# One wide product for high and low rows in the last wide expert of an attention, MoE and MLP kernel

## The chip, the core and the metric

The kernel runs on one core of a Trainium2 chip. The metric is the device time of one execution in microseconds (us). TensorE multiplies matrices and writes its results to PSUM; ScalarE and VectorE read PSUM and do the elementwise work; GpSimd issues the gathers and scatters; SyncE issues the weight loads. Each engine works through its own instructions in the order in which they were issued and waits on semaphores for the others.

## The reference

Attention over a window of 64 positions (2 batches, 8 heads, 576 positions, head size 64) gives 1152 rows of 512 values. Each row goes to the one of 8 experts that its gate chooses, then all rows go through a second MLP:

```python
logits = x @ w_gate
expert_idx = np.argmax(logits, axis=1)
...
h = np.maximum(np.einsum('ecd,edf->ecf', disp, w1), 0.0)
y = np.einsum('ecf,efd->ecd', h, w2)
...
out[i] = gate_w[i] * y[expert_idx[i], pos[i]]
```

```python
h = x @ w_in
g = np.maximum(h, 0.0) + alpha * np.minimum(h, 0.0)
return (g @ w_out).astype(np.float32)
```

An expert has 1024 hidden units and a capacity of 288 rows; the second MLP has 2048 hidden units. All arrays are float32. With the reference's own inputs the experts get, from the largest, 254, 234, 220, 194, 123, 74, 42 and 11 rows.

## The kernel before

**Numbers in two parts.** A float32 factor is held as a high part, rounded to the type `float32r`, and a low part, the remainder. A product of two such factors is the sum of three matmuls: high by high, high by low and low by high. `mm3` (L216) issues the three; `wide_up` writes its three out at L1092.

**Experts.** The experts are taken in an order of their size; `room` (L55) is how many rows each gets in the main path, and rows beyond that go to the part behind `tc.If(n_over > 0)` (L1439), which ends with a second pass of the second MLP. The experts with more than 128 rows of room are "wide" (positions 1, 3 and 7), the others "narrow"; positions 5 and 6 (`PAIR`) share one run of matmuls on unsplit weights. Position 7 (`HOST`, the fourth largest) is computed last, and the steps of the pair (the generator `pair`, L1237) run in between its own.

**A wide expert.** `halves_of` (L1160) turns its rows around into `xt`, high and low part, with columns for rows. `wide_up` (L1084) goes through four chunks of weights; a chunk has two blocks `f` of 128 hidden units, each the sum over four slices `kk` of three products. Both blocks of a chunk stand in one PSUM tile `hps` of the pool `ps_h` (two buffers, which `sps` of the narrow experts and `py` of the pair share). ScalarE makes the high part `hh` with a Relu out of PSUM (L1102), VectorE the low part `hl` (L1103). `wide_down` (L1112) sums four output blocks `y` over four chunks and two `f`; `put` (L1120) copies one block into its window of `x2`, the input of the second MLP: ScalarE casts the high part (L1121), VectorE subtracts for the low part (L1122). The window's place is known only at run time.

**Work issued in between.** The order of instructions is the order of the program (`tc.manual_schedule`). `prepare` (L1074) splits the next 128x1024 chunk of expert weights: a cast to `whi` (L1078, on ScalarE, each fourth one on VectorE) and a subtraction to `wlo` (L143, VectorE), after which the raw buffer is free and SyncE may issue the next load into it. `cvt_tick` (L193) does the same for a piece of the second MLP's weights, which come as pairs of 32-bit words: on ScalarE `mag` (L165) and a cast (L188), on VectorE L172, L173, L176 and L189. In `HOST` it is called after each chunk of `wide_up` and after the first three of `wide_down`; its first call that does anything is the one after chunk 2, and issues two `mag` activations, for the first two pieces. The later calls issue one tick each.

**Order in `HOST`.** Up: chunks 0 and 1; then the pair's `ptp` transposes, its `pps` products and their Relu (L1271); chunks 2 and 3; then `ptp` (L1251), its copy (L1253) and the first half of `py` (L1279). Down: output blocks 0 and 1 for chunks 0 and 1; the second half of `py`; blocks 0 and 1 for chunks 2 and 3; the pair's last transposes `ytp`, which go into two windows of `x2` (L1295 and L1296, one after the other for each window); `put(0)`, `put(1)`; block 2, `put(2)`; block 3, `put(3)`. Then the second MLP: `up` (L1362) forms `gps` from slices 0 to 3 of `x2` in turn, three products of 384 columns for each.

Of the kernel before, what the change touches and what calls it, by code (L numbers as in the profile page):

```python
# [7 lines left out]
F32 = mybir.dt.float32  # L8
F32R = mybir.dt.float32r
# [3 lines left out]
AF = mybir.ActivationFunctionType  # L13
ALU = mybir.AluOpType
# [12 lines left out]
def attention_moe_mlp_kernel(  # L27
# [13 lines left out]
    nc = tc.nc  # L41
# [10 lines left out]
    ORDER = (0, 1, 4, 2, 5, 6, 7, 3)  # L52
    HOST, PAIR = 7, (5, 6)
    WIDE, NARROW, HALF = min(cap, 256), 128, 64
    room = [min(cap, (NARROW, 240, 240, 240, NARROW, NARROW, HALF, HALF)[r]) for r in ORDER]  # L55
    NS = 2 * NE + 1
    NB = NS + 4 * NE
    MARK = 2048.0
# [157 lines left out]
    def mm3(ps, wa, xa, start, stop, cols=None):  # L216

        for n, (i, j) in enumerate(((0, 0), (0, 1), (1, 0))):
            nc.tensor.matmul(ps, wa[i], xa[j], start=start and n == 0, stop=stop and n == 2)  # L219

    with tc.manual_schedule():
        identf = const.tile([128, 128], F32, name="identf")
# [12 lines left out]
        with ExitStack() as es:  # L235
# [684 lines left out]
            last = NTILE - 1  # L920
# [93 lines left out]
        x2 = [x2p.tile([128, 4, XW], F32R, name=f"x2{n}") for n in "hl"]  # L1014
# [9 lines left out]
        with ExitStack() as es:  # L1024
# [56 lines left out]

            late = []

            def wide_up(p, xt, between=lambda c: None):  # L1084
                hT, at, n_ = [], first_part[p], room[p]
                for c in range(4):
                    hi, lo = (w.rearrange("p (k f) -> p k f", k=4) for w in parts.pop(at + c))
                    ps = ps_h.tile([128, 2, WIDE], F32, name="hps", tag="h")
                    for f in range(2):
                        fs = slice(128 * f, 128 * f + 128)  # L1090

                        for n, (i, j) in enumerate(((0, 0), (1, 0), (0, 1))):  # L1092
                            for kk in range(4):
                                nc.tensor.matmul(ps[:, f, :n_], (hi, lo)[i][:, kk, fs], xt[j][:, kk, :],  # L1094
                                                 start=n == kk == 0, stop=n == 2 and kk == 3)
                        while late and f:
                            late.pop(0)()
                        if f == 0:
                            prepare(at + c)
                    hh = hp.tile([128, 2, WIDE], F32R, name="hh", tag="hh")[:, :, :n_]  # L1100
                    hl = hp.tile([128, 2, WIDE], F32R, name="hl", tag="hl")[:, :, :n_]
                    nc.scalar.activation(out=hh, in_=ps[:, :, :n_], func=AF.Relu)  # L1102
                    nc.vector.scalar_tensor_tensor(hl, ps[:, :, :n_], 0.0, hh.bitcast(F32), op0=ALU.max,  # L1103
                                                   op1=ALU.subtract)
                    hT.append((hh, hl))
                    between(c)
                    prepare(at + c + 1)
                    if p == HOST:
                        cvt_tick(at + c - 1)
                return hT  # L1110

            def wide_down(p, win, hT, between=lambda c: None):  # L1112
                at = first_part[p] + 4
                ys = [ps_y.tile([128, WIDE], F32, name=f"y{d}", tag="y")[:, :room[p]] for d in range(4)]

                def part(c, f, d, hi, lo):
                    dd = slice(128 * d, 128 * d + 128)
                    mm3(ys[d], (hi[:, f, dd], lo[:, f, dd]), [x[:, f, :] for x in hT[c]], c == 0 and f == 0, c == 3 and f == 1)

                def put(d):  # L1120
                    nc.scalar.copy(x2[0][:, d, win], ys[d])  # L1121
                    nc.vector.tensor_tensor(x2[1][:, d, win], ys[d], x2[0][:, d, win].bitcast(F32), op=ALU.subtract)  # L1122

                if p == HOST:
                    w2 = []
# [33 lines left out]

            def halves_of(p):  # L1160
                tag, n_ = ("xw", WIDE) if room[p] > NARROW else ("xt", NARROW)
                xt = [xtp.tile([128, 4, n_], F32R, name=f"{tag}{n}", tag=f"{tag}{n}")[:, :, :room[p]] for n in "hl"]
                for h, tp in enumerate(turned(p)):
                    hi, lo = (x[:, :, 128 * h:min(room[p], 128 * h + 128)] for x in xt)
                    tp = tp[:, :, :min(128, room[p] - 128 * h)]
                    nc.scalar.copy(hi, tp)
                    nc.vector.tensor_tensor(lo, tp, hi.bitcast(F32), op=ALU.subtract)
                return xt

            def narrow(p, win, xt):  # L1170
                hts, pss, hT = {}, {}, {}
# [14 lines left out]
                def flip(n):  # L1186
                    tp = ps_x.tile([128, 4, 128], F32, name="stp", tag="x")
                    for f in range(4):
                        nc.tensor.transpose(tp[:, f, :], hts[n][:, 128 * f:128 * f + 128], identf)
                    hh = hp.tile([128, 4, 128], F32R, name="sh", tag="hh")  # L1190
                    hl = hp.tile([128, 4, 128], F32R, name="sl_", tag="hl")
                    nc.scalar.copy(hh, tp)
                    nc.vector.tensor_tensor(hl, tp, hh.bitcast(F32), op=ALU.subtract)
                    hT[n] = (hh, hl)
# [375 lines left out]
```

## Time and profile before

| | us |
|---|---|
| median of 3 runs | 400.74 |
| lowest and highest of them | 400.18, 404.31 |
| profiled execution | 401.88 |
| its span, first to last instruction | 400.1 |
| TensorE busy in it | 385.2 |
| VectorE busy in it | 284.7 |
| ScalarE busy in it | 198.0 |

The profile is of one execution. PE is TensorE's matmuls, PEld its weight loads, DVE is VectorE, ACT ScalarE, POOL GpSimd, SPq the queue of SyncE. Matmuls overlap each other: the length of one is not its price, the distance between two starts in a run of them is. A timeline row gives start, length, engine, line, what is written from what, and a count; in square brackets stands how long the engine stood idle before it, and what ended that. The chain of waits goes back from the last instruction, at each step to what released it or to the instruction before it on its engine.

### The profile page before, as it was taken

The numbers are of one execution on the slowest core, as the hardware profiler recorded it, in microseconds if no ns is written. First come the engines' busy times: TensorE is split into PE (matmuls) and PEld (weight loads), VectorE is DVE, ScalarE is ACT, GpSimd is POOL, SyncE is SP. The second block draws the span as 40 slices with busy tenths as digits, with TensorE's granted clock in tenths as the row PEclk, the third lists the DMA queues.
The fourth block names the chain that finished last, engine by engine and source line by source line (L and its number), as shares of the span: only waits on it lengthen the run. The fifth ranks groups of instructions, "written<-read, shape, count | busy, mean of one in ns | idle before, by whom it ended". The sixth has DMA issues, their size and how long they took to land.

```text
span 400.1 us, 8050 instructions
## 1 busy us (share of the span) xinstructions
PE 385.2 (96%) x2932; PEld 341.4 (85%) x2932; DVE 284.7 (71%) x686; ACT 198.0 (50%) x373; POOL 80.2 (20%) x287
## 2 busy tenths in 40 slices
PE   7999899999999999999999999999999999999990
PEld 4888786899989987867999889998899988999880
DVE  4778789699988754677699848999649963355220
ACT  4979555665756334444577646773137700354000
POOL 5543368422047830000000000000000000000441
PEclk9999999999999999999999999999999999999996
DMA  7772976999988654976133343343301000000221
GB/s 246 247 203 63 360 273 199 399 410 407 389 295 281 209 162 143 346 299 211 56 105 120 145 155 109 109 136 124 105 2 54 0 2 0 2 0 1 100 88 57
DMA packets 20447, 66.13 MB, mean 165 GB/s; under 512 B 2992, under 2 KB 2992, under 8 KB 20400
## 3 DMA queue, kind: packets, MB, share of 16 engines
q1 hardware_dynamic: 17728, 57.74, 41.3%
q0 software_dynamic: 2528, 7.53, 5.1%
q8 instruction: 25, 0.41, 0.5%
q10 hardware_dynamic: 144, 0.26, 0.2%
q14 instruction: 22, 0.18, 0.2%
HBM read 60.74 MB, written 4.79 MB: 164 GB/s over the span
## 4 chain that ended last, share of the span: by engine, by line
PE 85%; DVE 7%; DMA 2%; issue 2%; ACT 2%; POOLq 0%; another core or an unknown queue 0%; POOL 0%; ACTq 0%; DVEq 0%
PE gps L219 25%; PE ops L1397 25%; PE hps L1094 5%; PE y L219 5%; PE sy L219 4%; PE sps L219 3%; PE av L460 2%; PE sc L418 2%; PE tp L446 2%; PE pps L1264 2%; PE aps L763 2%; PE ay L774 2%; DMA raw<-mlp_in 1%; DVE wlo L143 1%; PE lg L486 1%
## 5 line engine op out<-in xcount | busy, mean ns | idle before, releaser
L219 PE MATMUL gps<-x2h,whi 128*128 128x384 f32 x192 | 64.3, 335 | 0.2 <-ACT x2h L1121 0.2
L219 PE MATMUL gps<-x2l,whi 128*128 128x384 f32 x192 | 64.3, 335 | 0.0
L219 PE MATMUL gps<-x2h,wlo 128*128 128x384 f32 x192 | 64.2, 334 | 0.0
L143 DVE TENSOR_TENSOR wlo<-raw,whi 128x1024 fp32r<-128x1024 f32 x45 | 53.8, 1222 | 13.0 <-ACT whi L1078 12.4
L1373 ACT ACTIVATE u<-gps,one 128x384 f32<-128x384 f32 x48 | 27.7, 577 | 59.0 <-PE gps L219 59.0
L1405 POOL DMA_INDIRECT out<-acc,tok x9 | 8.8, 974 | 238.7 <-DVE acc L1403 238.7
L1397 PE MATMUL ops<-whi,gl 128*128 128x512 f32 x144 | 56.1, 390 | 0.0
L1397 PE MATMUL ops<-wlo,gh 128*128 128x512 f32 x144 | 56.1, 390 | 0.0
L1397 PE MATMUL ops<-whi,gh 128*128 128x512 f32 x144 | 56.0, 389 | 0.0
L1403 DVE SCALAR_TENSOR_TENSOR acc<-ops,gate,acc 128x512 f32<-128x512 f32 x27 | 19.9, 748 | 33.1 <-PE ops L1397 33.1
L1374 DVE SCALAR_TENSOR_TENSOR g<-gps,slope,u 128x384 f32<-128x384 f32 x48 | 29.4, 612 | 19.0 <-ACT u L1373 18.9
L1078 ACT CAST whi<-raw 128x1024 fp32r<-128x1024 f32 x30 | 31.1, 1050 | 11.0 <-PE y L219 9.0
L219 PEld LDWEIGHTS gps<-x2h,whi 128*128 128x128 f32 x192 | 36.0, 188 | 0.5 <-ACT x2h L1121 0.4
L219 PEld LDWEIGHTS gps<-x2l,whi 128*128 128x128 f32 x192 | 36.0, 188 | 0.4 <-DVE x2l L1122 0.3
L219 PEld LDWEIGHTS gps<-x2h,wlo 128*128 128x128 f32 x192 | 36.0, 188 | 0.0
L1384 ACT ACTIVATE gh<-g,sign 128x384 fp32r<-128x384 f32 x48 | 29.3, 610 | 9.5 <-DVE g L1374 9.5
L1397 PEld LDWEIGHTS ops<-whi,gl 128*128 128x128 f32 x144 | 27.0, 188 | 5.7
L1397 PEld LDWEIGHTS ops<-wlo,gh 128*128 128x128 f32 x144 | 27.0, 188 | 5.5
L1397 PEld LDWEIGHTS ops<-whi,gh 128*128 128x128 f32 x144 | 27.0, 188 | 5.5
L1385 DVE SCALAR_TENSOR_TENSOR gl<-g,sign,gh 128x384 fp32r<-128x384 f32 x48 | 29.2, 608 | 0.2 <-ACT gh L1384 0.2
L189 DVE TENSOR_TENSOR wlo<-w,whi 128x512 fp32r<-128x512 f32 x32 | 21.9, 686 | 9.4 <-ACT whi L188 9.4
L188 ACT CAST whi<-w 128x512 fp32r<-128x512 f32 x32 | 19.6, 612 | 16.9 <-DVE w L176 16.9
(285 smaller groups left out, 828.2 us busy)
## 6 DMA issues: line engine op xcount, KB each, us to landing
raw<-moe_in SPq DMA_DIRECT2D x61, 512.0 KB
raw<-mlp_in SPq DMA_DIRECT2D x32, 512.0 KB
v<-v_in SPq DMA_DIRECT2D x8, 260.0 KB
sw<-moe_in SPq DMA_DIRECT2D x4, 512.0 KB
qT<-q_in SPq DMA_DIRECT2D x6, 256.0 KB
kT<-k_in SPq DMA_DIRECT2D x5, 256.0 KB
qT<-q_in SPq DMA_DIRECT2D x2, 384.0 KB
kT<-k_in SPq DMA_DIRECT2D x2, 384.0 KB
```

Source lines behind the costliest of these rows:

```text
L143: eng.tensor_tensor(lo, raws.pop(split[c]), hi.bitcast(F32), op=ALU.subtract)
L188: nc.scalar.copy(hi, w)
L189: nc.vector.tensor_tensor(lo, w, hi.bitcast(F32), op=ALU.subtract)
L219: nc.tensor.matmul(ps, wa[i], xa[j], start=start and n == 0, stop=stop and n == 2)
L1078: (nc.vector.tensor_copy if c % 4 == 3 else nc.scalar.copy)(ring_tiles(c)[0], raws[split[c]])
L1094: nc.tensor.matmul(ps[:, f, :n_], (hi, lo)[i][:, kk, fs], xt[j][:, kk, :], start=n == kk == 0, stop=n == 2 and kk == 3)
L1373: nc.scalar.activation(out=u, in_=ps, func=AF.Copy, scale=one[:, ft:ft + 1])
L1374: nc.vector.scalar_tensor_tensor(g, ps, slope[:, ft:ft + 1], u, op0=ALU.mult, op1=ALU.max)
L1384: nc.scalar.activation(out=gh, in_=g, func=AF.Copy, scale=sg)
L1385: nc.vector.scalar_tensor_tensor(gl, g, sg, gh.bitcast(F32), op0=ALU.mult, op1=ALU.subtract)
L1397: nc.tensor.matmul(ps, a_[:, ts_], b_[:, f % 2, :], start=f == 0 and n == 0, stop=f == 3 and n == 2)
L1403: nc.vector.scalar_tensor_tensor(acc[:, tt, :], ps, sc, acc[:, tt, :], op0=ALU.mult, op1=ALU.add)
```

## The change

Only `HOST` changes its arithmetic. Where the high weights met the high and the low rows in two products, they now meet both in one product that writes the two halves of a PSUM tile; the low weights add theirs to the first half. ScalarE and VectorE then add the halves (`total`) into a tile `sums` in SBUF, from which Relu and the subtraction, or the two steps of `put`, read. `ps_h` now gives one tile for each `f` of `HOST` rather than one for each chunk. The room of the expert goes from 240 to 200 rows. `xt` and the hidden values become one tile each for high and low part, in all experts.

```diff
--- before.py
+++ after.py
@@ -52,7 +52,7 @@
     ORDER = (0, 1, 4, 2, 5, 6, 7, 3)
     HOST, PAIR = 7, (5, 6)
     WIDE, NARROW, HALF = min(cap, 256), 128, 64
-    room = [min(cap, (NARROW, 240, 240, 240, NARROW, NARROW, HALF, HALF)[r]) for r in ORDER]
+    room = [min(cap, (NARROW, 240, 240, 200, NARROW, NARROW, HALF, HALF)[r]) for r in ORDER]
     NS = 2 * NE + 1
     NB = NS + 4 * NE
     MARK = 2048.0
@@ -217,6 +217,17 @@
 
         for n, (i, j) in enumerate(((0, 0), (0, 1), (1, 0))):
             nc.tensor.matmul(ps, wa[i], xa[j], start=start and n == 0, stop=stop and n == 2)
+
+    def mm_both(ps, hi, lo, x, first, last):
+
+        def low():
+            nc.tensor.matmul(ps[:, 0, :], lo, x[:, 0], start=False, stop=False)
+
+        if not first:
+            low()
+        nc.tensor.matmul(ps, hi, x, start=first, stop=last)
+        if first:
+            low()
 
     with tc.manual_schedule():
         identf = const.tile([128, 128], F32, name="identf")
@@ -1081,28 +1092,40 @@
 
             late = []
 
+            def total(out, ps):
+                nc.scalar.copy(out, ps[:, 0, :])
+                nc.vector.tensor_tensor(out, out, ps[:, 1, :], op=ALU.add)
+
             def wide_up(p, xt, between=lambda c: None):
                 hT, at, n_ = [], first_part[p], room[p]
                 for c in range(4):
                     hi, lo = (w.rearrange("p (k f) -> p k f", k=4) for w in parts.pop(at + c))
-                    ps = ps_h.tile([128, 2, WIDE], F32, name="hps", tag="h")
+                    hb = hp.tile([128, 2, 2, WIDE], F32R, name="hb", tag="hb")[:, :, :, :n_]
+                    if p == HOST and c == 0:
+                        sums = xtp.tile([128, 2, 2, WIDE], F32, name="sums", tag="xt")
+                    hh, hl = hb[:, 0], hb[:, 1]
+                    if p != HOST:
+                        ps = ps_h.tile([128, 2, WIDE], F32, name="hps", tag="h")[:, :, :n_]
                     for f in range(2):
                         fs = slice(128 * f, 128 * f + 128)
-
-                        for n, (i, j) in enumerate(((0, 0), (1, 0), (0, 1))):
+                        if p == HOST:
+                            ps = ps_h.tile([128, 2, WIDE], F32, name="hps", tag="h")[:, :, :n_]
                             for kk in range(4):
-                                nc.tensor.matmul(ps[:, f, :n_], (hi, lo)[i][:, kk, fs], xt[j][:, kk, :],
-                                                 start=n == kk == 0, stop=n == 2 and kk == 3)
+                                mm_both(ps, hi[:, kk, fs], lo[:, kk, fs], xt[:, :, kk, :], kk == 0, kk == 3)
+                            total(sums[:, c % 2, f, :n_], ps)
+                        else:
+                            for n, (i, j) in enumerate(((0, 0), (1, 0), (0, 1))):
+                                for kk in range(4):
+                                    nc.tensor.matmul(ps[:, f, :], (hi, lo)[i][:, kk, fs], xt[j][:, kk, :],
+                                                     start=n == kk == 0, stop=n == 2 and kk == 3)
                         while late and f:
                             late.pop(0)()
                         if f == 0:
                             prepare(at + c)
-                    hh = hp.tile([128, 2, WIDE], F32R, name="hh", tag="hh")[:, :, :n_]
-                    hl = hp.tile([128, 2, WIDE], F32R, name="hl", tag="hl")[:, :, :n_]
-                    nc.scalar.activation(out=hh, in_=ps[:, :, :n_], func=AF.Relu)
-                    nc.vector.scalar_tensor_tensor(hl, ps[:, :, :n_], 0.0, hh.bitcast(F32), op0=ALU.max,
-                                                   op1=ALU.subtract)
-                    hT.append((hh, hl))
+                    pre = sums[:, c % 2, :, :n_] if p == HOST else ps
+                    nc.scalar.activation(out=hh, in_=pre, func=AF.Relu)
+                    nc.vector.scalar_tensor_tensor(hl, pre, 0.0, hh.bitcast(F32), op0=ALU.max, op1=ALU.subtract)
+                    hT.append(hb)
                     between(c)
                     prepare(at + c + 1)
                     if p == HOST:
@@ -1111,15 +1134,24 @@
 
             def wide_down(p, win, hT, between=lambda c: None):
                 at = first_part[p] + 4
-                ys = [ps_y.tile([128, WIDE], F32, name=f"y{d}", tag="y")[:, :room[p]] for d in range(4)]
+                ys = [ps_y.tile([128, 2, WIDE], F32, name=f"y{d}", tag="y")[:, :, :room[p]] for d in range(4)]
+                sums = xtp.tile([128, 2, 2, WIDE], F32, name="sums", tag="xt") if p == HOST else None
 
                 def part(c, f, d, hi, lo):
                     dd = slice(128 * d, 128 * d + 128)
-                    mm3(ys[d], (hi[:, f, dd], lo[:, f, dd]), [x[:, f, :] for x in hT[c]], c == 0 and f == 0, c == 3 and f == 1)
+                    ends = c == 0 and f == 0, c == 3 and f == 1
+                    if p == HOST:
+                        mm_both(ys[d], hi[:, f, dd], lo[:, f, dd], hT[c][:, :, f, :], *ends)
+                    else:
+                        mm3(ys[d][:, 0, :], (hi[:, f, dd], lo[:, f, dd]), [hT[c][:, n, f, :] for n in range(2)], *ends)
 
                 def put(d):
-                    nc.scalar.copy(x2[0][:, d, win], ys[d])
-                    nc.vector.tensor_tensor(x2[1][:, d, win], ys[d], x2[0][:, d, win].bitcast(F32), op=ALU.subtract)
+                    y = ys[d][:, 0, :]
+                    if p == HOST:
+                        y = sums[:, d // 2 % 2, d % 2, :room[p]]
+                        total(y, ys[d])
+                    nc.scalar.copy(x2[0][:, d, win], y)
+                    nc.vector.tensor_tensor(x2[1][:, d, win], y, x2[0][:, d, win].bitcast(F32), op=ALU.subtract)
 
                 if p == HOST:
                     w2 = []
@@ -1159,13 +1191,14 @@
 
             def halves_of(p):
                 tag, n_ = ("xw", WIDE) if room[p] > NARROW else ("xt", NARROW)
-                xt = [xtp.tile([128, 4, n_], F32R, name=f"{tag}{n}", tag=f"{tag}{n}")[:, :, :room[p]] for n in "hl"]
+                both = xtp.tile([128, 2, 4, n_], F32R, name=tag, tag=tag)[:, :, :, :room[p]]
+                xt = [both[:, 0], both[:, 1]]
                 for h, tp in enumerate(turned(p)):
                     hi, lo = (x[:, :, 128 * h:min(room[p], 128 * h + 128)] for x in xt)
                     tp = tp[:, :, :min(128, room[p] - 128 * h)]
                     nc.scalar.copy(hi, tp)
                     nc.vector.tensor_tensor(lo, tp, hi.bitcast(F32), op=ALU.subtract)
-                return xt
+                return both if p == HOST else xt
 
             def narrow(p, win, xt):
                 hts, pss, hT = {}, {}, {}
@@ -1187,8 +1220,8 @@
                     tp = ps_x.tile([128, 4, 128], F32, name="stp", tag="x")
                     for f in range(4):
                         nc.tensor.transpose(tp[:, f, :], hts[n][:, 128 * f:128 * f + 128], identf)
-                    hh = hp.tile([128, 4, 128], F32R, name="sh", tag="hh")
-                    hl = hp.tile([128, 4, 128], F32R, name="sl_", tag="hl")
+                    hb = hp.tile([128, 2, 4, 128], F32R, name="sh", tag="hb")
+                    hh, hl = hb[:, 0], hb[:, 1]
                     nc.scalar.copy(hh, tp)
                     nc.vector.tensor_tensor(hl, tp, hh.bitcast(F32), op=ALU.subtract)
                     hT[n] = (hh, hl)
```

## Rows read from the trace of the kernel before

**Rows 1.** The page, part 1: span; busy us (share of span) xinstructions.

```profile
span 400.1 us, 8050 instructions
...
PE 385.2 (96%) x2932; PEld 341.4 (85%) x2932; DVE 284.7 (71%) x686; ACT 198.0 (50%) x373; POOL 80.2 (20%) x287
```

**Rows 2.** Chain of waits, 150 to 200 us: start us, us, what.

```profile
168.76 1.24 DVE wlo L143
...
170.01 4.69 DMA raw<-mlp_in
...
175.40 0.57 ACT hh L1102
...
175.99 0.66 DVE hl L1103
...
190.32 0.43 DVE x2l L1296
...
190.77 0.39 ACT x2h L1295
...
191.18 0.44 DVE x2l L1296
...
191.64 0.37 ACT x2h L1121
```

**Rows 3.** Timeline of TensorE, 172 to 200 us, in `HOST` and after it.

```profile
172.48 0.60 PE L1251 MATMUL ptp<-identf,spht 128*128 128x128 f32 x4
173.01 3.65 PE L1279 MATMUL py<-raw,sphTp 128*64 128x512 f32 x16
...
191.58 0.27 PE L219 MATMUL y<-hh,wlo 128*128 128x240 f32 x1
192.05 0.44 PE L219 MATMUL gps<-x2h,whi 128*128 128x384 f32 x1 [0.20 <-ACT x2h L1121]
...
194.52 0.33 PE L219 MATMUL gps<-x2h,whi 128*128 128x384 f32 x1
```

**Rows 4.** Chain of waits of the whole span: start us, us, runs of matmuls.

```profile
61.27 4.29 PE ay L774 x10
...
128.80 10.72 PE y L219 x96
...
242.09 24.98 PE gps L219 x144
267.07 24.52 PE ops L1397 x108
```

**Rows 5.** Groups of instructions by line and shape: xcount, busy us, mean ns, idle before.

```profile
L1103 DVE SCALAR_TENSOR_TENSOR hl<-hps,hh 128x480 fp32r<-128x480 f32 x12 | 7.8, 651 | 1.9 <-ACT hh L1102 1.1 <-issue 0.8
...
L1122 DVE TENSOR_TENSOR x2l<-y,x2h 128x240 f32 x12 | 4.1, 399 | 0.4 <-ACT x2h L1121 0.4
L1121 ACT CAST x2h<-y 128x240 f32 x12 | 3.9, 365 | 2.0 <-PE y L219 1.5 <-DVE x2l L1296 0.5
```

**Rows 6.** Timelines of ScalarE and of VectorE in `HOST`: 156 to 196 us.

```profile
173.58 0.68 ACT L165 ACTIVATE mag<-raw 128x512 f32<-128x512 f32 x1 [1.58 <-DMA raw<-mlp_in]
174.81 0.69 ACT L165 ACTIVATE mag<-raw 128x512 f32<-128x512 f32 x1 [0.55 <-DMA raw<-mlp_in]
...
191.64 1.15 ACT L1121 CAST x2h<-y 128x240 f32 x4 [0.49 <-DVE x2l L1296]
...
192.03 1.35 DVE L1122 TENSOR_TENSOR x2l<-y,x2h 128x240 f32 x4 [0.43 <-ACT x2h L1121]
```

**Rows 7.** Stretches of 0.5 us at the end: us, busy us of engines, PEclk, DMA, GB/s.

```profile
390.50:391.00 0.50, 0.11 (x1) 0.00 (x0) 0.36 (x1) 0.00 (x0) 0.00 (x0) 1.00 1.02 393
...
393.00:393.50 0.50, 0.00 (x0) 0.00 (x0) 0.00 (x0) 0.00 (x0) 0.00 (x0) 1.00 0.68 238
393.50:394.00 0.50, 0.00 (x0) 0.00 (x0) 0.00 (x0) 0.00 (x0) 0.00 (x0) 0.89 0.69 262
394.00:394.50 0.50, 0.00 (x0) 0.00 (x0) 0.00 (x0) 0.00 (x0) 0.00 (x0) 0.50 0.06 25
```

## The prediction

> **What bounds the kernel now.** I read the page first: TensorE is busy 96% of the span [rows 1], which would make TensorE time the thing to save. That share is an average, so I looked next at the stage the change edits, the last wide expert, `HOST`, in the chain of waits [rows 2]. There the reader sees that the piece released last is not a matmul. The chain runs from VectorE's `wlo` L143, which frees a weight buffer, through the transfer of a second-MLP weight piece (170.01 to 174.70) and ScalarE and VectorE work without a break to 192.05, where the first matmul of the second MLP starts. Everything between 175.99 and 190.32 is VectorE and ScalarE in turns: the weight conversions that `cvt_tick` issues, each engine in the order of the program. The timeline of TensorE [rows 3] shows the other side: its last `y` matmul starts at 191.58, so TensorE ends some 0.1 us later and waits only about 0.35 us. Two chains end almost together; TensorE work saved here is worth 0.4 us at most before the other chain alone counts, and VectorE or ScalarE work added to that chain counts in full.
>
> **Part by part.** *TensorE's products.* Before, a unit (one 128-row slice of weights for one output block) is three products of 240 columns at 10.72/96 = 0.1117 us, 0.335 us [rows 4]. After, it is one of 400 and one of 200. No row has these widths. Between 384 columns (24.98/144 = 0.1735) and 512 (24.52/108 = 0.2270) a column costs 0.418 ns, which puts 400 at 0.180. For 200 that line gives 0.097 and the nearest row, 240 columns, 0.112; I take 0.112. A unit becomes 0.292 and saves 0.043 us (0.058 by the other bound). There are 32 units in `wide_up` and 32 in `wide_down`: 1.38 us each, 2.8 us in all (3.7).
>
> *What `total` adds.* A 240-column ScalarE copy out of PSUM takes 0.365 us and a 480-column one 0.57 [rows 2, 5], 0.87 ns a column: 0.33 for 200. VectorE's 240 take 0.399 and 480 take 0.651 [rows 5], 1.05 ns a column: 0.36 for 200. `wide_up` gets eight of each and `wide_down` four of each. Relu and `hl` shrink from 480 to 400 columns: 0.50 and 0.57. They now read SBUF; I leave that unpriced, since it concerns four instructions. A handover between the two engines costs 0.02 to 0.03 (191.18 + 0.44 to 191.64) [rows 2]. Instructions of one engine overlap by about 0.1 us: four casts take 1.15, four subtractions 1.35 [rows 6], 0.26 and 0.32 apart.
>
> *The first three chunks of `wide_up`.* Their sums and adds sit among the `prepare` casts, and TensorE, now with one PSUM tile per `f` from two buffers, will wait here and there for an add. I cost this at nothing: ScalarE stands idle 1.58 us before 173.58 and 0.55 before 174.81, both times for a transfer [rows 6], and that is the cover. The transfer that lands at 174.8 starts when L143 ends at 170.0 [rows 2]; that subtraction follows the pair's relu, which follows TensorE's `pps`, so it should move by no more than 0.3 us. If the cover were gone, the three chunks would add 6 x 0.28 less 3 x 0.08 = 1.4 us of VectorE time.
>
> *The fourth chunk.* Both `L165` activations of the first tick are issued after chunk 2, so on ScalarE they stand in front of chunk 3's copies. In the kernel before only `hh` of chunk 3 stood behind them (175.40) and TensorE had no need of it yet. After: copy of f=0 at 175.40 to 175.73, its add 175.76 to 176.12; copy of f=1 from 175.64, its add from 176.05 to 176.41; Relu from 176.44 to 176.94; `hl` from 176.97 instead of 175.99. Since `hl` is 0.08 shorter, everything behind it on VectorE is 0.90 late: conversions, `L1296`, the casts.
>
> *TensorE's new wait.* `py`, the pair's second product, takes the oldest of the two `ps_h` buffers. Before, that was chunk 2's tile, long read, and `py` started at 173.01 [rows 3]. After, it is the tile of chunk 3, f=0, whose add ends at 176.12. TensorE is done with chunk 3 and the four transposes `ptp` at about 172.9 and stands still until 176.15, some 3.2 us; `py`, all of `wide_down` and the second MLP are queued behind it. From there the rest took 18.68 us (173.01 to 191.69) and saves 1.38: it ends at 193.45, 1.8 later than before, and both halves of the saving are gone.
>
> *The four `put`s.* `L1296` starts at 190.32 + 0.90 = 191.22; with the second `L1295` and `L1296` behind it, VectorE can take the first add at 191.22 + 0.86 + 0.35 = 192.43 [rows 2]. Add to 192.79, cast `x2h` 192.81 to 193.14, `x2l` from 193.16. On VectorE the next add comes behind `x2l`: a round is 0.33 + 0.02 + 0.28 + 0.36 + 0.03 = 1.02 us, where it was 0.3 before. So the casts come at 192.81, 193.83, 194.85, 195.87, and the last `x2l` ends at 195.87 + 0.35 + 0.36 = 196.58. The second MLP's first group reads the four slices in this order; its products 10 to 12 take the last slice. Product 11 starts at about 196.6, and product 13 two steps on (0.28 and 0.17), at 197.05; before it started at 194.52 [rows 3].
>
> *Sum.* 197.05 - 194.52 = 2.5 us more. Behind it both TensorE and VectorE are as much later and the second MLP keeps its pace. Narrower tiles in `halves_of` and the merged `xw`, `xt`, `hb` tiles are hidden: their shares alternate between experts as before and TensorE has other products meanwhile. The profiled execution took 401.88 us (span 400.1), so by its own time 404.4. It lies 1.14 above the median of the three runs, 400.74; against that the forecast is **403.2 us**, 0.6% more. About 1%, 4.0 us, is what a measurement of this kernel can tell from no change.
>
> A rule that speaks against the change: the new wide product writes two runs of 200 columns, 256 apart, and every `y` and `gps` row above writes one run, so no row prices it [rows 4]. The Trainium skill (PSUM — Partial Sum Buffer, Specifications (TRN2)) says that any non-contiguous access pattern slows matmuls significantly, without a figure. No run here shows it so far; what it would do is the third rival.
>
> **The rivals.** *The saving counts.* If the two transfers land earlier, ScalarE never stands before chunk 3's copies, TensorE does not stop, and it ends at 193.45 - 3.2 = 190.25; one `put` behind it (0.15 + 0.36 + 0.39 + 0.36 + 0.38) and the last two steps (0.45) give 192.35 for product 13, 2.2 us sooner: 398.5. It decides from a landing 2.5 us before 174.8 on. For it: TensorE and some buffers are free earlier. Against it: the transfer starts at the end of L143 [rows 2], which hardly moves. 0.18, most of it with a part of the gain, around 401.
>
> *TensorE's clock falls in its wait.* At the end of the run TensorE has 0.11 us of work left after 390.50; the granted clock is still full (1.00, 2.4 GHz) until about 393.9 and then goes to the lower level, 1.2 GHz [rows 7]. So rest does bring it down here. Whether the stop of 3.2 us that I forecast does, no row of before shows, since the longest waits in this stage are tenths of a us. If it falls, the price is between nothing and `py` at half speed, 3.6 us more [rows 3]: TensorE would end at 197.05, and with the same tail product 13 starts at 199.2, 4.7 later: 405.4. This is the one that ends on the slower side; it decides from some 2.5 us of loss on. Against it: the stop is shorter than the rest after which the rows show the drop. 0.12.
>
> *Products with two runs are slow.* The slowest matmul row per column, `ay`, has 4.29/10 = 0.429 us for 512 columns [rows 4], 0.84 ns each: 400 would take 0.335, a unit 0.447, 0.155 more than forecast. In `wide_down` alone that is 5.0 us, all behind the stop; with a part of `wide_up`'s five, through `pps` and L143, about 6 to 8 over the forecast, 410. For it only that nothing like it is in the trace. 0.07.
>
> *It doesn't do what it says.* If more than 200 rows went to this expert, the overflow path at the end would run and repeat the second MLP, some 200 us. The fourth largest expert of the reference's inputs gets 194. 0.01.
>
> **How the numbers follow.** Forecast 0.62, with 402 to 405 as its own range (the handovers, the size of a round, runs of before from 400.18 to 404.31). The range 400.0 to 406.0 takes in the upper half of the first rival and all of the second. Slower by over 1% (above 404.75): 0.06 of the forecast, 0.08 of the second rival, 0.07 and 0.01: 0.22. Faster by over 1% (below 396.7): 0.02, the far end of the first rival. The rest, 0.76, is within 1%.
>
> **What would show it.** Right: `py` starts near 176.1 after a stop of about 3 us; chunk 3's copies stand right behind the second `L165`; `L1296` starts near 191.2; four `put`s about 1 us apart; the first group of the second MLP has three pauses; a 400-column product starts its successor 0.18 us later. Wrong: TensorE without a stop before `py`, transfers that land before 173, `L1296` before 190.5, or a step of 0.3 us behind the wide product.

## The result and the profile after

| | before | after |
|---|---|---|
| median of 22 runs, us | 400.68 | 403.12 |
| lowest and highest, us | 399.48, 404.31 | 401.70, 405.17 |
| profiled execution, us | 401.88 | 402.73 |

The ratio is 1.0066 with a 95% interval of 1.005 to 1.0083: 2.4 us slower, on a forecast of 403.2. That is within the 1% that the prediction took for no change, but the interval excludes 1.

The first part of the page of the kernel after answers to [rows 1]. TensorE is busy 0.8 us less, VectorE 3.2 and ScalarE 2.7 us more, and the sum is a slower kernel:

```profile
span 401.0 us, 7944 instructions
...
PE 384.4 (96%) x2867; PEld 338.6 (84%) x2868; DVE 287.9 (72%) x698; ACT 200.7 (50%) x385; POOL 78.9 (20%) x287
```

The chain of waits of the kernel after, 150 to 200 us (start, us, what), answers to [rows 2]:

```profile
169.03 4.35 DMA raw<-mlp_in
...
173.49 0.04 ACT mag L165
...
174.06 0.32 ACT sums L1096
174.40 0.65 DVE sums L1097 x2
175.07 0.55 ACT hb L1126
175.64 0.57 DVE hb L1127
...
189.88 0.43 DVE x2l L1329
190.33 0.38 ACT x2h L1328
190.74 0.31 DVE x2l L1329
191.08 0.36 DVE sums L1097
191.47 0.37 ACT x2h L1153
191.86 0.34 DVE x2l L1154
...
193.60 0.37 ACT x2h L1153
193.97 0.04 issue
194.01 1.02 PE gps L219 x3
```

It runs over the same transfer and the same conversions as before. Two pieces are new: behind the activation that waited for the transfer (`mag`, 173.49) stand chunk 3's copies, adds and Relu, and at the end each `put` is a round of add, cast and subtraction through both engines. The timeline of TensorE of the kernel after, 170 to 197 us, answers to [rows 3] (in brackets the idle time before, and what ended it):

```profile
171.79 0.60 PE L1284 MATMUL ptp<-identf,spht 128*128 128x128 f32 x4
...
174.82 3.65 PE L1312 MATMUL py<-raw,sphTp 128*64 128x512 f32 x16 [2.42 <-DVE sums L1097]
...
187.82 0.36 PE L228 MATMUL y<-hb,whi 128*128 128x400 f32 x1
...
191.94 0.37 PE L228 MATMUL y<-hb,whi 128*128 128x400 f32 x1
192.14 0.34 PE L219 MATMUL gps<-x2h,whi 128*128 128x384 f32 x1
...
192.95 0.44 PE L219 MATMUL gps<-x2h,whi 128*128 128x384 f32 x1
...
194.01 0.44 PE L219 MATMUL gps<-x2h,whi 128*128 128x384 f32 x1
...
195.08 0.44 PE L219 MATMUL gps<-x2h,whi 128*128 128x384 f32 x1
...
195.94 0.35 PE L219 MATMUL gps<-x2h,whi 128*128 128x384 f32 x1
```

TensorE stands 2.42 us before `py`. The rows at 192.14, 192.95, 194.01 and 195.08 start the four slices of the second MLP's first group. The first stands right behind the last product of `HOST` (191.94); the other three wait for their casts, 1.06 us apart. The row at 195.94 is product 13, the first behind the four.

Two executions do not reach this stage at the same moment, so product 13 is taken below from two marks inside the execution. **From S**, the first `pps` product (the first row is of before, the second of after): 41.15 before (153.37 to 194.52), 43.28 after (152.66 to 195.94), 2.13 more.

```profile
153.37 3.67 PE L1264 MATMUL pps<-raw,xp 128*64 128x256 f32 x32
152.66 3.67 PE L1297 MATMUL pps<-raw,xp 128*64 128x256 f32 x32
```

**From L**, the second `L165` of the first tick, which waits for the second transfer: 19.71 before (174.81 to 194.52) and 22.45 after (173.49 to 195.94), 2.74 more. They differ because the transfer stood 0.6 us earlier against S in this execution of after. One execution can't give this closer: in the eleven profiles of this document that keep L, S to L takes 20.63 to 21.99 us. Behind product 13 nothing changes: the last matmul starts 195.7 us behind it in both.

### The profile page after: what moved, and what is told of

Same layout as the page of the kernel before. It is cut to its first block, busy times and chain, and to the rows that moved or that the text cites. A ratio compares the mean times of both kernels' runs of the same rounds, so it can differ in the third digit from the quotient of the medians.

```text
span 401.0 us, 7944 instructions
## 1 busy us (share of the span) xinstructions
PE 384.4 (96%) x2867; PEld 338.6 (84%) x2868; DVE 287.9 (72%) x698; ACT 200.7 (50%) x385; POOL 78.9 (20%) x287
## 4 chain that ended last, share of the span: by engine, by line
PE 69%; DMA 12%; DVE 9%; ACT 4%; issue 3%; POOL 1%; SPq 1%; POOLq 0%; DVEq 0%; ACTq 0%
PE gps L219 25%; PE ops L1430 24%; DMA raw<-moe_in 7%; PE sy L219 3%; PE y L219 3%; PE sps L219 2%; DVE wlo L143 2%; PE av L471 2%; PE sc L429 2%; PE hps L1119 1%; PE tp L457 1%; DMA v<-v_in 1%; DMA xe<-xr,sl 1%; PE lg L497 1%; DMA raw<-mlp_in 1%
```

## The experiments

The theory: the end of the stage is set by the chain of VectorE and ScalarE, lengthened by chunk 3's queue (0.9 us) and by the rounds of the `put`s (1.6 us). The first rival: the stop of TensorE before `py` sets it. The second: the clock falls in that stop.

| kernel | median, us | before on that chip | ratio [95%] | over before: forecast, measured | 13th from S | 13th from L |
|---|---|---|---|---|---|---|
| before (profile) | | | | | 41.15 | 19.71 |
| after | 403.12 | 400.68 | 1.0066 [1.005, 1.0083] | 2.5, 2.44 | 43.28 | 22.45 |
| up_only | 403.86 | 400.54 | 1.008 [1.0053, 1.0106] | 2.4, 3.32 | 45.02 | 23.71 |
| down_only | 402.28 | 400.54 | 1.0039 [1.0021, 1.0058] | 1.6, 1.74 | 43.75 | 21.76 |
| room_only | 400.16 | 400.54 | 0.9987 [0.9966, 1.0007] | within 0.5, -0.38 | 40.76 | 19.49 |
| tick_late | 404.25 | 400.54 | 1.0088 [1.0055, 1.0121] | 1.6, 3.71 | 44.10 | |
| tail_woven | 405.50 | 402.17 | 1.0084 [1.0055, 1.0113] | 1.1, 3.33 | 42.21 | 21.11 |
| tick_out | 404.56 | 402.17 | 1.0065 [1.0035, 1.0095] | 1.0, 2.39 | 43.19 | 22.56 |
| before_tick_out | 402.28 | 402.17 | 0.9994 [0.9968, 1.002] | -0.4 to 0, 0.11 | 40.65 | 19.01 |
| all_three | 400.84 | 402.17 | 0.9962 [0.9938, 0.9985] | -2.2, -1.33 | 39.75 | |
| py_elsewhere | 405.72 | 402.12 | 1.0082 [1.0054, 1.011] | 2 to 3.5, 3.60 | 44.21 | 22.49 |
| after_busy | 405.42 | 402.12 | 1.0075 [1.0046, 1.0105] | 2.0, 3.30 | 44.43 | 22.45 |
| woven_busy | 403.67 | 402.12 | 1.0036 [1.0014, 1.0057] | 1.1 to 1.4, 1.55 | 42.72 | 21.10 |
| late_woven | 404.11 | 402.12 | 1.006 [1.0037, 1.0082] | 0.3 to 1.0, 1.99 | 42.40 | |

Kernels with the same time of before ran on the same chip. Where the mags were moved there is no L to count from. Most of the forecasts are too low, those of `tick_late`, `tail_woven`, `tick_out`, `after_busy` and `late_woven` by about a us or more.

### The parts alone

`up_only` takes `wide_down` and `put` back, `down_only` takes `wide_up` back, `room_only` is the kernel before with the smaller room.

```diff
 # up_only, against after
...
-                    if p == HOST:
+                    if False:
                         mm_both(ys[d], ...
...
-                    if p == HOST:
+                    if False:
                         y = sums[:, d // 2 % 2, d % 2, :room[p]]
```

```diff
 # down_only, against after: one tile for each chunk, three products, no total
...
-                        if p == HOST:
-                            ps = ps_h.tile([128, 2, WIDE], F32, name="hps", tag="h")[:, :, :n_]
...
-                            total(sums[:, c % 2, f, :n_], ps)
...
-                    pre = sums[:, c % 2, :, :n_] if p == HOST else ps
+                    pre = ps
...
```

```diff
 # room_only, against before
-    room = [min(cap, (NARROW, 240, 240, 240, NARROW, ...
+    room = [min(cap, (NARROW, 240, 240, 200, NARROW, ...
```

> The change in wide_up alone; wide_down and its puts as before, room 200. Theory (TensorE's stop before py and the late fourth chunk cost by themselves): the stop of about 2.5 to 3.2 us stays, TensorE saves only 1.4 in wide_up, which the stop eats; about 403.0, 2.4 over before. Rival 'only the four puts cost': no more than 0.5 over before. Rival 'the loss lies in the narrower room or the merged tiles': as the whole change, 403, but without a stop.

> The change in wide_down alone; wide_up with three products and one PSUM tile for a chunk as before, room 200. Theory: no stop before py, TensorE ends 1.4 us earlier, but four put rounds of 1.05 us hang behind the conversions on VectorE: about 402.3, 1.6 over before. Rival 'only the stop costs': 399.3, 1.4 under before.

> The kernel before with 200 rows of room instead of 240 and nothing else. Theory: TensorE's products get shorter by at most 0.015 us each, but VectorE's conversions set the start of the second MLP: within 0.5 us of before, rather below. Rival 'TensorE's time counts': up to 2.9 us under before. Rival 'the room itself costs': 403.

`room_only` can't be told from before. Its products of 200 columns stand 0.111 us apart (5.34 us for 48) where 240 took 0.1117 [rows 4]: fewer columns at this width save nothing, as the prediction chose.

`down_only` has no stop, and its first `x2l` of the pair stands 15.35 us behind L, where it stood 15.51 before. What it loses is in the tail alone: 21.76 - 19.71 = 2.05 by the profile. Of this 0.35, by the working below, goes to a clock that fell, which its stretches of 1 us show (busy us of PE, PEld, DVE, ACT, POOL; PEclk; DMA share; GB/s):

```profile
192.00:193.00 1.00, 0.95 (x4) 0.42 (x4) 0.57 (x3) 0.52 (x3) 0.00 (x0) 0.90 0.00 0
193.00:194.00 1.00, 1.00 (x3) 0.73 (x3) 0.57 (x3) 0.47 (x2) 0.00 (x0) 0.50 0.00 0
194.00:195.00 1.00, 1.00 (x5) 0.88 (x4) 0.90 (x6) 0.00 (x0) 0.00 (x0) 0.50 0.00 0
```

From the first `x2l` to product 13 it took 6.41 us, at full clock in the kernel after 6.06. That leaves 1.70: 1.86 for the tail (6.06 less the 4.20 of before) and 0.16 less ahead of it. The prediction's own tail is 2.5 - 0.9 = 1.6.

`up_only` loses more than the whole change. The reason stands in its timeline of TensorE and in its stretches (columns as above):

```profile
175.52 5.35 PE L1311 MATMUL py<-raw,sphTp 128*64 128x512 f32 x16 [2.91 <-DVE sums L1097]
```

```profile
175.00:176.00 1.00, 0.48 (x3) 0.20 (x5) 0.63 (x2) 0.53 (x3) 0.00 (x0) 1.00 0.66 164
176.00:177.00 1.00, 1.00 (x6) 0.39 (x4) 0.67 (x2) 1.00 (x3) 0.00 (x0) 0.63 0.82 274
177.00:178.00 1.00, 1.00 (x4) 0.24 (x2) 0.97 (x2) 0.88 (x2) 0.00 (x0) 0.50 0.50 201
178.00:179.00 1.00, 1.00 (x4) 0.24 (x2) 1.00 (x2) 0.00 (x0) 0.00 (x0) 0.50 0.02 8
```

After a stop of 2.91 us the granted clock is down to 1.2 GHz (0.50) from about 176.3 to 179.7, and `py` takes 5.35 us instead of 3.65. With short `put`s and the saving of `wide_down` gone, TensorE is the bound here: from the first `gps` at 195.79 to product 13 at 197.90 it has no pause. So the stop and the 1.7 us count in full. This is the second rival at work, in this kernel.

### Does the stop matter in the changed kernel?

`py_elsewhere` gives `py` a buffer of another pool, so that it need not wait for chunk 3's add.

```diff
-                y = ps_h.tile([128, D], F32, name="py", tag="h")
+                y = ps_x.tile([128, D], F32, name="py", tag="x")
```

> The changed kernel with py in a buffer of the pool ps_x, which does not wait for chunk 3's add; nothing else. Theory (VectorE's chain sets the start of the second MLP by itself): no stop before py, TensorE ends 3 us earlier and then waits in front of the second MLP instead; product 13 no earlier than 0.3 us against the changed kernel, and with the clock falling in that wait 2 to 3.5 over before. Rival 'the stop before py costs the time': 0.5 over before or less.

Its timeline of TensorE has no stop before `py`, and a wait in front of the second MLP instead:

```profile
172.84 3.65 PE L1312 MATMUL py<-raw,sphTp 128*64 128x512 f32 x16
...
193.34 0.45 PE L219 MATMUL gps<-x2h,whi 128*128 128x384 f32 x1 [1.13 <-ACT x2h L1153]
...
197.39 0.34 PE L219 MATMUL gps<-x2h,whi 128*128 128x384 f32 x1
```

Product 13 stands 22.49 us behind L (174.90), with the stop 22.45. TensorE gets to the second MLP earlier and waits there. The stop doesn't set product 13 in this kernel; the first rival falls. The timed runs are 3.6 us over before, where that rival had 0.5 at most. This is more than the kernel after has (2.44): seven of the twelve runs are listed with a granted clock below 0.991 and have a median of 405.98, the other five 403.87, 2.04 over before's runs of such clocks (401.83). Where the clock fell in the seven, no trace shows; the profiled execution has full clock.

### Taking the chain's two pieces away

`tick_late` puts the two mags behind chunk 3. `tail_woven` issues each block's copy and add when the block is ready, between the products of the next ones, so that behind the last product stand one add and the last casts and subtractions. `tick_out` leaves the last tick of `wide_down` to the second MLP, which takes it off VectorE here; `before_tick_out` does the same to the kernel before, as a control.

```diff
 # tick_late, against after
-                    if p == HOST:
-                        cvt_tick(at + c - 1)
+                    if p == HOST and c == 3:
+                        cvt_tick(at + c - 1)
+                        cvt_tick(at + c - 1)
```

```diff
 # tail_woven, against after; added(d) is total() alone, put(d, y) the two steps behind it
...
-                        if d == 0:
-                            continue
                         if d == 1:
+                            sum_of = [added(0), added(1)]
+                        elif d == 2:
                             late.pop(0)()
-                            put(0)
-                        put(d)
+                            sum_of.append(added(2))
+                            put(0, sum_of[0])
+                            put(1, sum_of[1])
+                        elif d == 3:
+                            sum_of.append(added(3))
+                            put(2, sum_of[2])
+                            put(3, sum_of[3])
```

```diff
 # tick_out, against after; before_tick_out, against before
                         between(c)
-                        cvt_tick(at - 1)
+                        if c < 2:
+                            cvt_tick(at - 1)
```

> The changed kernel with the first conversion tick moved from behind chunk 2 to behind chunk 3 (two ticks there), so that ScalarE has chunk 3's copies in front of the activations that wait for the transfers. Theory: no stop before py, TensorE ends 3 us earlier, the fourth chunk's 0.9 us of delay goes; the four put rounds stay: about 402.3, 0.9 under the changed kernel. Rival 'the stop alone costs': 398.5. Rival 'only the puts cost': 403.2.

> The changed kernel with the adds of the output blocks issued ahead of the subtractions of earlier blocks, and blocks 0 and 1 added before the pair's last casts; same work in another order. Theory: the stop before py stays, the rounds of 1.05 us shrink, so that product 13 of the second MLP comes about 1.4 us sooner than in the changed kernel: 401.8. Rival 'the stop alone costs': no change, 403.1.

> The changed kernel without the conversion tick behind chunk 2 of wide_down; the second MLP takes it over, whose VectorE has room. Theory: VectorE reaches the puts 3.2 us earlier, only the last put stands behind TensorE, which still ends late by its stop: 401.7, 1.0 over before. Rival 'only the puts cost, and TensorE's saving counts once VectorE is free': 398.5. Rival 'the second MLP has no room for the tick': no better than 403.

> The kernel before without that tick, a control. Theory: TensorE's chain is 0.4 us behind VectorE's here, so at most 0.4 under before: 400.4. Rival 'the second MLP has no room for the tick': 402 to 403.

> The changed kernel with all three edits: first tick behind chunk 3, woven puts, and without the tick behind chunk 2 of wide_down. Theory: neither the stop nor VectorE holds TensorE, so both halves of its saving count, less one put behind the last block: 398.5, 2.2 under before. Rival 'something else in the change costs': still above 400.7.

**tick_late** is a miss: 404.25, not below the kernel after but above. The stop before `py` is gone (0.25 us), yet nothing is won. The timeline of VectorE of `tick_late` shows why:

```profile
171.46 1.23 DVE L143 TENSOR_TENSOR wlo<-raw,whi 128x1024 fp32r<-128x1024 f32 x1 [0.36 <-ACT whi L1089]
...
173.83 0.58 DVE L1127 SCALAR_TENSOR_TENSOR hb<-sums,hb 128x400 fp32r<-128x400 f32 x1 [0.60 <-ACT hb L1126]
...
175.04 1.23 DVE L143 TENSOR_TENSOR wlo<-raw,whi 128x1024 fp32r<-128x1024 f32 x1
176.19 0.42 DVE L172 TENSOR_SCALAR w<-raw 128x512 int32<-128x512 int32 x1
...
177.44 0.69 DVE L176 SCALAR_TENSOR_TENSOR w<-mag,w 128x512 int32<-128x512 int32 x1
```

In the kernel after, VectorE does the first tick's L172, L173 and L176 (172.28 to 174.2) in the time before chunk 3's sums are there. Here they come behind chunk 3 and two conversions, at 176.19, and VectorE hardly pauses before that. Its own load replaced the transfer as what comes last, and the first `x2l` of the pair stands 37.70 us behind S, after 37.22 in the kernel after. The wait for the transfer wasn't idle time for the engine that mattered.

**tail_woven** moves product 13 to 21.11 behind L, 1.34 less than after, as meant. Its timeline of TensorE has the second MLP begin without a wait and go on without a pause:

```profile
193.26 0.44 PE L219 MATMUL gps<-x2h,whi 128*128 128x384 f32 x1
...
195.69 0.33 PE L219 MATMUL gps<-x2h,whi 128*128 128x384 f32 x1
```

And yet its median is 1.0084 of before's: the profile's gain isn't in the median. The next section takes this up.

**tick_out** is like `up_only`: without the tick TensorE is the bound, its stop of 2.22 us brought the clock down (0.70, 0.50, 0.50 and 0.59 in the four stretches of 1 us from 176), and `py` took 5.35. The first row is of `tick_out`, the second of `tail_woven`, where the clock stayed full:

```profile
176.37 5.35 PE L1313 MATMUL py<-raw,sphTp 128*64 128x512 f32 x16 [2.22 <-DVE sums L1097]
175.91 3.65 PE L1319 MATMUL py<-raw,sphTp 128*64 128x512 f32 x16 [2.70 <-DVE sums L1097]
```

Less that 1.7, product 13 would stand 20.86 behind L, 1.15 over before.

**before_tick_out** is within 0.3% either way, so the tick alone is worth nothing that can be measured.

**all_three** has all three edits, and is a little faster than before, by 0.4%: 400.84 against 402.17 on its chip, ratio 0.9962 [0.9938, 0.9985]. The kernel after, on another chip, had 1.0066. Its timeline of TensorE:

```profile
173.67 3.65 PE L1321 MATMUL py<-raw,sphTp 128*64 128x512 f32 x16 [0.26 <-DVE sums L1097]
...
190.99 0.43 PE L219 MATMUL gps<-x2h,whi 128*128 128x384 f32 x1
...
193.43 0.33 PE L219 MATMUL gps<-x2h,whi 128*128 128x384 f32 x1
```

From S product 13 is at 39.75, 1.40 less than before; 2.8 was what the products save by the forecast. A wait of 0.7 us before chunk 3, for a buffer of `ps_h`, and 0.26 before `py` are left.

### Is the clock part of the loss?

`after_busy` and `woven_busy` fill the stop with 20 products that nobody reads; `late_woven` has `tick_late` and `tail_woven` together, so that there is no stop to fill.

```diff
 # after_busy, against after; woven_busy, against tail_woven
                 flip(1)
+                idle = ps_x.tile([128, 512], F32, name="idle2", tag="x")
+                fill = identf.bitcast(BF16)
+                for _ in range(20):
+                    nc.tensor.matmul(idle[:, :256], fill[:, :128], fill[:, :256], start=True, stop=True)
                 y = ps_h.tile([128, D], F32, name="py", tag="h")
```

> The changed kernel with 20 products of 256 columns on the identity matrix put in front of py, some 2.2 us of TensorE work that nobody reads, inside the stop. Theory (part of the changed kernel's 2.4 us is TensorE's clock, which falls in the stop in some executions and then costs py up to 1.7 us): the stop shrinks to about half a us, the clock stays up behind it, about 2.0 over before. Rival 'the clock is not part of it': 2.4 over before, or more by the added work.

> The changed kernel with the woven puts and the same 20 products in front of py. Theory: the weaving was worth its 1.1 us in the profile (product 13 of the second MLP) and lost it to the clock that fell in the stop; with the stop filled, 1.1 to 1.4 over before. Rival 'the woven order itself costs in the timed runs': 3.3 over before, as without the products.

> The changed kernel with the first tick behind chunk 3 and the woven puts, but with all ticks in place. Theory: TensorE no longer stops before py, and VectorE comes to the puts as late as in the kernel before; woven rounds are about 0.5 us longer in all than the old puts; 0.3 to 1.0 over before, more where the clock falls in front of the second MLP. Rival 'order is enough, VectorE's load is not the limit': 1.5 under before, as with all three edits.

`woven_busy` stands at 1.0036 where `tail_woven`, with the same 21.1 us from L, stood at 1.0084. `after_busy` gave 1.0075, no better than after: a miss. Its 20 products took 2.35 us and left 1.39 us of the stop (1.04 in `woven_busy`). `late_woven`, at 1.006, is a miss too: its TensorE waits 2.52 us in front of `gps`, for `x2h`, as VectorE is again the one that comes last. By themselves these are ratios of different chips. But each timed run lists its mean granted clock, and this says more. The runs of `tail_woven` and of the kernel after, sorted by it (clock, us; of after the median of each group):

```
tail_woven  0.982 407.90   0.982 408.07   0.983 405.94   0.983 406.82   0.985 406.12   0.986 405.35
            0.986 405.64   0.990 404.20   0.990 404.31   0.990 404.41   0.991 403.69   0.994 402.94
after       0.983 to 0.988: 404.23 (8 runs)   0.989 to 0.991: 402.74 (5)   0.992 to 0.994: 402.73 (9)
```

A listed clock counts the end of the span too. The profiles of before and of `room_only` have full clock until after their last matmul and are listed at 0.992 and 0.991. So from 0.991 to 0.995 a run need not have had a fall.

Compared among such runs, at 0.991 and above, `tail_woven` (2 of 12, median 403.31) is 1.55 over before (22 of 35, 401.76), and `woven_busy` (8 of 12, 403.36) 1.53 over (19 of 32, 401.83). Their profiles say 1.40 and 1.39 from L. Two runs are few, but at like clock the times agree with the profiles. Ten of the twelve runs of `tail_woven` have a lower clock, and its median lies higher with them. `all_three` (8 of 12, 400.70) is 1.1 under before at like clock; its profile has 1.40 from S.

Where the clock fell, a listed mean doesn't say. By the line through its runs `tail_woven` loses 0.39 us for each 0.001 of clock (0.001 is about 0.4 us of TensorE's time in a span of 400). But before's own runs on these two chips lose 0.30 and 0.24, go down to 0.983 as well, and there is no stop in this stage to blame. Three profiles show a fall far ahead of it, in the attention part. Here is `after_busy` (listed at 0.989), the timeline of TensorE from 36 to 48 us and then the stretches, columns as above:

```profile
43.26 0.84 PE L487 MATMUL tx<-identf,xr 128*128 128x128 f32 x4 [1.10 <-DVE xr L481]
```

```profile
43.00:44.00 1.00, 0.74 (x5) 0.77 (x6) 0.51 (x4) 0.33 (x1) 0.71 (x4) 0.77 1.01 385
44.00:45.00 1.00, 1.00 (x7) 0.67 (x7) 0.86 (x5) 0.27 (x2) 0.00 (x0) 0.50 1.02 414
```

The clock is down from about 43.5 to 47 us, and full through the whole of `HOST`. `tick_out` and the control `before_tick_out` have a fall at the same place, behind a stop of 1.34 us; before has such a stop there, 1.35 us, and keeps full clock. So for the chips of `tail_woven` and `woven_busy` it stays open how much of the lower clock belongs to the stop before `py`.

On the chip of `up_only` it is plainer. The 27 runs of before and the 12 of `room_only` lay at 0.991 to 0.995. `up_only` had 7 of 10 at 0.988 to 0.990, with a median of 404.1 us, and three at 0.993 or above, with 402.2; `down_only` had 5 of 12 and `tick_late` 5 of 6 at 0.987 or 0.988. The profiled execution of each is one of the low ones and has its fall in this stage. There the stop and the waits that come with the edits brought the clock down.

In the kernel after, the nine runs at 0.992 or above have a median of 402.73, 2.05 over before's 400.68; the median of all is 2.44 over. Before's clocks on this chip weren't kept, so this sets chosen runs against all. That some 0.4 us of the loss goes with a lower clock, here or elsewhere in the span, would fit and is not shown: the profile of after has the full clock through the stage. What a fall in its stop would cost can be estimated. `py` takes 1.70 us longer (`up_only`), so TensorE would come to the second MLP at 192.14 + 1.70 = 193.84; twelve products without a pause take 2.11 us (`up_only`), which puts product 13 at 195.95, and it stands at 195.94. By this estimate the rounds of the `put`s hide such a fall, and the second rival isn't what makes this kernel slower.

## Why the prediction was right, point by point

**What bounds the stage.** Right: chains of ScalarE and VectorE, not TensorE's 96%. `py_elsewhere` shows it most plainly, as a TensorE that isn't stopped ends up in the same place.

**The products.** A unit went from 0.335 to 0.294 us (187.82 to 191.94 are 14 units, 4.12 us); 0.292 was predicted. The rival of slow two-run products falls. Only the sum came out: the next start comes about 0.20 us behind a product of 400 columns and about 0.09 behind one of 200, where 0.18 and 0.11 were forecast. The Trainium skill (PSUM — Partial Sum Buffer, Specifications (TRN2)) says that any non-contiguous access pattern slows matmuls significantly. This trace doesn't bear it out for two runs of 200 columns: 0.294 us for the unit, against 0.292 from rows that write single runs.

**The new instructions.** The groups by line and shape of the kernel after (count, busy us, mean ns, idle before):

```profile
L1126 ACT ACTIVATE hb<-sums 128x400 fp32r<-128x400 f32 x4 | 2.2, 538 | 4.5 <-DVE sums L1097 4.5
...
L1153 ACT CAST x2h<-sums 128x200 f32 x4 | 1.4, 360 | 2.0 <-DVE sums L1097 2.0
L1097 DVE TENSOR_TENSOR sums<-sums,y 128x200 f32<-128x200 f32 x4 | 1.4, 354 | 0.0
L1096 ACT COPY sums<-y 128x200 f32<-128x200 f32 x4 | 1.3, 322 | 0.0
```

Copy 0.32 (predicted 0.33), add 0.35 (0.36). The Relu took 0.54 and the cast 0.36, where 0.50 and 0.33 were predicted from rows that read PSUM; these read SBUF, which I had left unpriced.

**Chunk 3.** Its copies stand behind the second `L165`, as predicted. From L to `hl` it is 2.15 us instead of 1.18, 0.97 more (0.98), and the pair's first `x2l` comes 0.88 later (0.90). The first three chunks cost nothing that shows: from S to L it is 20.83 us, before 21.44, well inside the 20.63 to 21.99 of the profiles, with one wait of TensorE of 0.7 us for a buffer.

**The stop.** It is there, for the reason given, but 2.42 us and not 3.2. `py` starts 1.33 after L (1.34 predicted), so the term was right and its start was off: the transfer stood 0.6 us earlier against S in this execution, and TensorE was done with `ptp` 0.2 later than assumed. `up_only` had 2.91, `tail_woven` 2.70. That TensorE would end 1.8 later could not decide anything: `py_elsewhere`, without the stop, has the same 22.49.

**The rounds.** 1.06 us instead of 1.02, mostly through the slower cast. From the pair's first `x2l` to product 13 it takes 6.06 against 4.20 before, 1.86 more where 1.63 was forecast. Chain and rounds make 2.74 from L (2.5 predicted). This is the term that was a little small.

**The time.** 403.2 was forecast on 2.5 us of longer chain. The profile has 2.13 from S and 2.74 from L, the timed runs 2.44. The mechanism and its two terms, 0.9 and 1.6, came out as 0.88 and 1.86. That the median is right to 0.1 us is partly luck: the profiles give the chain no closer than some 0.6, and the base was a median of three runs between 400.18 and 404.31 (400.74, where 22 runs gave 400.68).

**The rivals.** The saving that counts (0.18) needed a transfer 2.5 us sooner; it came 0.6 sooner. The fall of the clock got 0.12, and that was too little as a statement on this stage: it came down in the profiled stops of `up_only` and `tick_out`, and I had argued against it from the end of the run, where the rows still show full clock 3 us after the last work [rows 7]. Its price was too high: `py` took 1.70 us longer and not 3.6, and to count at all it would have needed TensorE to be the bound.

## What to carry to other kernels

An engine that works 96% of the span need not set the end of a stage: follow the chain through the stage, and count what the change adds to the engines on it, a queue's head that waits for a transfer included. Work added at the end of a stage counts with its round trips (1.06 us for 200 columns through two engines); the same adds issued as soon as their operand was ready left no pause behind them in the profile (`tail_woven`). An order that takes a wait away is won only when no engine takes over as the last, and three edits that each gained nothing in the median alone (`tick_late`, `tail_woven`, `tick_out`) gained together, by 0.4% over before; of the pairs only `late_woven` was run, which gained nothing either. A mean clock of a run doesn't say in which stage the clock fell; a profile by stretches does.

## What the hardware showed

TensorE's granted clock fell to 1.2 GHz after stops of 2.91 (`up_only`) and 2.22 us (`tick_out`), and stayed full after 2.42 (the kernel after) and 2.70 (`tail_woven`): the length of a stop alone doesn't decide it. It fell as well in the short pauses in front of the second MLP, after a wait of 1.15 us and two pauses of tenths (`down_only`, stretches above) or one (`tick_late`), and not in `py_elsewhere` after 1.13 and three. In the attention part it fell after 1.34 us in `before_tick_out` and not after 1.35 in before. Within the runs of `tail_woven` the time followed the listed clock, 402.9 at 0.994 to 408.1 at 0.982. And a wide matmul that writes two separate runs of 200 columns, with the one of 200 columns beside it, took 0.294 us, what rows of single runs gave for the two.
